# Fused sliding-window attention and squared-ReLU MLP on one core: first up-projection group in 128-token pieces, weights loaded between the first blocks, more transposes through the DMA

## Chip, cores, metric

The kernel runs on one core of a Trainium2 chip. The metric is device time in microseconds (us) of that core. Every kernel was run several times; executions of one kernel mostly agree within 1%, and all ratios here are of runs in the fast state (an execution over 1.5% above the fastest of its kernel counts as slow). A ratio is the mean time of one kernel's fast runs over the mean of the fast runs of the kernel before in the same rounds on the same chip, so it is not quite the ratio of the medians that are quoted beside it.

## The reference, cut to what matters

```python
# q, k, v: (8 batches, 8 heads, 576 tokens, 64) float32
scores = q @ k.T / 8
bias   = slope[h] * -abs(i - j)             # ALiBi
mask   = (i - j >= 0) & (i - j < 128)       # sliding window
attn   = softmax(where(mask, scores + bias, -1e9)) @ v
x = attn.transpose(0, 2, 1, 3).reshape(4608, 512)
h = maximum(x @ w_in, 0) ** 2               # w_in  (512, 2048)
out = h @ w_out                             # w_out (2048, 512), float32 out
```

## The kernel before

The program works on 40 attention blocks (8 batches of 576 tokens: four blocks of 128 and one of 64) and on 9 MLP groups of 512 tokens. A block needs k and q with the head dimension on the partitions (`kqT`), and its result x with the model dimension on the partitions (`xT`). Both turns can be done in two ways: on TensorE (eight 128x128 transposes for k and q, four for x, then copies out of PSUM), or by a DMA transpose that SyncE issues. Two constants choose the way by block number. A planner in Python, with its own estimates of durations, fixes one static order of instructions; on the chip each engine runs its list in that order and stops where an operand is missing.

```python
FIRST = "b0 b1 b2 b3 b4 i0 i1 i2 i3 b5 b6 b7 b8 b9 o0 o1 o2 o3"   # order of the first loads
SPLIT = [(0, 512)]           # pieces of group 0's up-projection
KQ_DMA, X_DMA = 10, 13       # from these blocks on, k/q and x are turned by DMA
size = {"kq": 4, "v": 6, "kqT": 5, "P": 3, "x": 3}                  # ring sizes
# [...]
def load_block(m, key):      # k, q, v of a block: float32 -> bf16, from GpSimd's queue
    # [...]
    nc.gpsimd.dma_start(o, src[b, :, kb * 128:kb * 128 + n, :].rearrange("h s d -> s h d"))
# [...]
if kq_by_dma:                # turn(m)
    nc.sync.dma_start_transpose(kqT[sk.idx], kq[s_in[m, "k"].idx].rearrange("s t f -> s (t f)"))
else:                        # 8 TensorE transposes of 128x128, two copies
    nc.tensor.transpose(slot.tile[:, i * 128:(i + 1) * 128], kq[...][:, i // C, ...], ident)
# [...]
if x_by_dma:                 # mix(m)
    nc.sync.dma_start_transpose(xT[:, :, t0:t0 + n], xt[sx.idx][0:n, :])
else:                        # 4 TensorE transposes, one copy
    nc.tensor.transpose(slot_x.tile[:, c * 128:(c + 1) * 128], xt[sx.idx][:, ...], ident)
```

The loads of all blocks are issued in block order from GpSimd.

The softmax here doesn't subtract the row's maximum and nothing guards it: scores larger than these inputs give would overflow.

Of the kernel before, what the change touches and what calls it, by code (L numbers as in the profile page):

```python
# [14 lines left out]
class Task:  # L15


    __slots__ = ("engs", "key", "emit", "deps", "acq", "rel", "nout", "users",
                 "ready", "start", "end", "eng", "seq", "lat", "dma")

# [16 lines left out]
class Plan:  # L37
# [18 lines left out]
    def order(self):  # L56
        used = {tag: [] for tag in self.bufs}
        free = {}
        cand = {}
        left = {}  # L60
# [12 lines left out]
        def avail(t):  # L73
            at = t.ready
            more = {}
            for s in t.acq:
                if s.idx is not None:
                    continue
                u = used[s.tag]
                n = self.bufs[s.tag]  # L80
                more[s.tag] = more.get(s.tag, 0) + 1
                i = len(u) + more[s.tag] - 1 - n
                if i >= 0:
                    old = u[i]
                    if old.left:
                        return None
                    at = max(at, old.freed)
            return at

        done = []  # L90
        n_all = len(self.tasks)
        while len(done) < n_all:
# [20 lines left out]
            if t.dma is not None:  # L113
                at = max(st + dur + 900.0, self.dma_free)
                self.dma_free = at + t.dma
                t.end = self.dma_free + 900.0
            else:
                t.end = st + dur + (self.LAT[e] if t.lat is None else t.lat)
            free[e] = st + dur
            for x in t.engs:  # L120
# [21 lines left out]
def kernel(  # L142
# [17 lines left out]

    FIRST = "b0 b1 b2 b3 b4 i0 i1 i2 i3 b5 b6 b7 b8 b9 o0 o1 o2 o3"
    SPLIT = [(0, 512)]

    KQ_DMA, X_DMA = 10, 13

# [3 lines left out]

    ident = const.tile([128, 128], BF16)  # L170
    masks = const.tile([128, H, 2, 128], BF16)
    pair_masks = const.tile([128, H, 256], BF16)
# [9 lines left out]


    size = {"kq": 4, "v": 6, "kqT": 5, "P": 3, "x": 3}
    kq = ring("kq", size["kq"], [128, 2, d_model])
# [16 lines left out]


    def build_iota():
        nc.gpsimd.iota(dist, pattern=[[-128, 2], [1, 128]], base=128, channel_multiplier=-1,
                       allow_small_or_imprecise_dtypes=True)

    t_iota = plan.add({"POOL": 360.0}, -9e5 + 0.012, build_iota)

    def build_ident():  # L210
        nc.vector.tensor_single_scalar(ident, dist[:, 1], 0.0, op=ALU.is_equal)

    t_ident = plan.add({"DVE": 230.0}, -9e5 - 1, build_ident, [t_iota])

# [19 lines left out]

    def build_pair():
        nc.vector.tensor_copy(pair_masks[:, :, 0:128].rearrange("p h (t s) -> p h t s", t=2), masks[:, :, :, 0:64])
        nc.vector.tensor_copy(pair_masks[:, :, 128:256], masks[:, :, 1, :])
        nc.vector.memset(kqT[NKB - 1][:, 0:C, 64:128], 0.0)

    t_pair = plan.add({"DVE": 1300.0}, -9e5 + 9, build_pair, t_mask)  # L240

    def ones():
        for t in vt:
            nc.vector.memset(t[:, :, D:D + 1], 1.0)
        for t in vt[NKB - 1:]:
            nc.vector.memset(t[64:128, :, 0:D], 0.0)
    t_ones = plan.add({"DVE": 1200.0}, -9e5 + 1, ones)


    def load(key, ns, emit, deps=(), acq=()):  # L250
        return plan.add({"POOL": 900.0}, key, emit, deps, acq, dma=ns)
# [21 lines left out]
    def load_block(m, key):  # L273
        b, kb = divmod(m, NKB)
        n = blk[kb]
        s_in[m, "k"] = s_in[m, "q"] = Slot("kq")
        s_in[m, "v"] = Slot("v")
        for i, (nm, src) in enumerate((("k", k), ("q", q), ("v", v))):
            sl = s_in[m, nm]

            def emit(i=i, src=src, sl=sl, nm=nm):
                o = (vt[sl.idx][0:n, :, 0:D] if nm == "v"
                     else kq[sl.idx][0:n, i].rearrange("s (h d) -> s h d", h=H))
                nc.gpsimd.dma_start(o, src[b, :, kb * 128:kb * 128 + n, :].rearrange("h s d -> s h d"))  # L284
            t_in[m, nm] = load(key + 0.01 * i, 1050.0 * n / 128, emit, [t_ones] if nm == "v" else [], [sl])

# [15 lines left out]
    def where(m):  # L302
        b, kb = divmod(m, NKB)
        return b, kb, blk[kb], (b * S + kb * 128 + blk[kb]) / 4 - 192 - 40, b == 0

    def turn(m):
# [7 lines left out]
        if kq_by_dma:  # L314
            def turn_kq():
                nc.sync.dma_start_transpose(kqT[sk.idx], kq[s_in[m, "k"].idx].rearrange("s t f -> s (t f)"))
            t_kq = [plan.add({"SP": 1300.0}, due - 80, turn_kq, [t_in[m, "k"], t_in[m, "q"]], [sk],
                             [s_in[m, "k"]], dma=1300.0)]
        else:
            slot = Slot("h" if first else "a")  # L320
            last = None
# [20 lines left out]
    def score(ms):  # L342
# [36 lines left out]
        for i in range(4):  # L379
            def view(t):  # L380
                if pair:
                    return t
                return t.rearrange("p c (t q) -> p c t q", t=2)[:, :, lo // 128:2, 0:n]

            def Pv(i=i):
                return view(Pt[sP.idx][:, 2 * i:2 * i + 2].rearrange("p h t q -> p h (t q)"))

            def expo(i=i):
                nc.scalar.activation(Pv(i), view(slot_s[i].tile.rearrange("p (c x) -> p c x", c=2)),  # L389
                                     AF.Exp, bias=0.0, scale=scale)  # L390
            cols = 2 * sum(w[2] for w in work_of)
            te = plan.add({"ACT": act(cols)}, due - 28 + 3 * i, expo, [tm], [], [slot_s[i]])

            def mask(i=i):
                pt = Pv(i)
                mk = (pair_masks if pair else masks.rearrange("p h t q -> p h (t q)"))[:, 2 * i:2 * i + 2]
                nc.vector.tensor_tensor(pt, pt, view(mk), op=ALU.mult)  # L397
            t_P.append(plan.add({"DVE": dve(cols, 2)}, due - 28 + 3 * i, mask,
                                [te] + (([t_pair] if pair else t_mask))))

    def mix(m):
# [57 lines left out]
        else:  # L459
            slot_x = Slot("h" if first else "a")  # L460
            last = None
# [31 lines left out]

    def fc_step(g, fc, key, lo=0, hi=512):
        if g not in g_slots:
            g_slots[g] = Slot("g")
            g_sq[g] = [[] for _ in range(FCB)]
        sg = g_slots[g]
        slot = Slot("o" if g == 0 and fc % 2 else "h")
        last = None  # L500
        w = hi - lo
        for cc in range(C):
            def emit(cc=cc, slot=slot):
                if cc == 0:
                    slot.tile = psum.tile([128, 512], FP32, tag=slot.tag, name="h")
                nc.tensor.matmul(slot.tile[:, 0:w], w_in_sb[:, cc, fc * 128:(fc + 1) * 128],  # L506
                                 xT[:, cc, g * 512 + lo:g * 512 + hi], start=cc == 0, stop=cc == C - 1)
            last = plan.add({"PE": mm(w)}, key + cc * w / 512, emit,
                            [last, t_win[fc // 4]] + tokens(g * 512 + lo, g * 512 + hi),
                            [slot, sg] if cc == 0 else [])  # L510
        srt = Slot("rt")

        def relu(slot=slot, srt=srt):
            srt.tile = work.tile([128, 512], BF16, tag="rt", bufs=3, name="rt")
            nc.scalar.activation(srt.tile[:, 0:w], slot.tile[:, 0:w], AF.Relu, bias=0.0, scale=1.0)  # L515
        tr = plan.add({"ACT": act(w)}, key, relu, [last], [srt], [slot])

        def square(srt=srt):
            if sg.tile is None:
                sg.tile = work.tile([128, FCB, 512], BF16, tag="g", bufs=2, name="g")  # L520
            nc.vector.tensor_tensor(sg.tile[:, fc, lo:hi], srt.tile[:, 0:w], srt.tile[:, 0:w], op=ALU.mult)  # L521
        g_sq[g][fc].append(plan.add({"DVE": dve(w, 2)}, key, square, [tr], [], [srt]))

    o_slots = {}

    def t_part(g, t, part, key):
# [4 lines left out]
        for fc in range(4 * part, 4 * part + 4):  # L531
            def emit(fc=fc):
                if fc == 0:
                    slot.tile = psum.tile([128, 512], FP32, tag="o", name="o")
                nc.tensor.matmul(slot.tile, sg.tile[:, fc, t * 128:(t + 1) * 128], w_out_sb[:, fc, :],  # L535
                                 start=fc == 0, stop=fc == FCB - 1)
            last = plan.add({"PE": mm(512)}, key + fc % 4, emit, [last, t_wout[fc // 4]] + g_sq[g][fc],
                            [slot] if fc == 0 else [], [sg] if t == 3 and fc == FCB - 1 else [])
        o_slots[g, t][1] = last
        if part == 3:  # L540
# [14 lines left out]
            plan.add({"SP": 350.0}, key, store, [te], [], [so])  # L555

    key = 0
    for lo, hi in SPLIT:
        for fc in range(FCB):
            fc_step(0, fc, key, lo, hi)  # L560
            key += 4 * (hi - lo) / 512
    for g in range(NG):
        for u in range(16):
            if g + 1 < NG:
                fc_step(g + 1, u, key)
                key += 4
            t_part(g, u // 4, u % 4, key)
            key += 4

    done = plan.order()  # L570
    kernel.plan = done
    with tc.manual_schedule():
# [32 lines left out]
```

## Time and profile before

| | before |
|---|---|
| time, median | 320.3 us |
| span of the profiled run | 318.9 us |
| first up-projection matmul | 24.05 us |
| last matmul starts | 314.7 us |
| TensorE idle after 40 us, by the waits | 0.8 us |

The waits of TensorE after 40 us (who waited, for whom, us in total, times, longest), kernel before:

```profile
PE h L506 <- DMA xT<-x: 0.6, 1, 0.6
PE xp L466 <- DVE x L447: 0.2, 1, 0.2
```

The DMA view of 40 to 140 us, kernel before: queue, packets, MB, share of the 16 engines (GpSimd's loads are `software_dynamic`, SyncE's stores and transposes `hardware_dynamic`); and for the DMA transposes the count and the median us from issue to landing:

```profile
q0 software_dynamic: 56860, 8.57, 137.2%
q1 hardware_dynamic: 22858, 7.90, 47.0%
...
kqT<-kq SPq DMA_TRANSPOSE x17, 6.3
...
xT<-x SPq DMA_TRANSPOSE x9, 6.3
```

A sum that is not a view of the profile is used below too: each matmul of the trace counted at its full-clock spacing as the trace shows it in full stretches (215.7 ns for 512 columns, 82 for 192, 56 for 128, 34 for a score of 128 columns, 30 for a P-times-v matmul; warm-up matmuls count as nothing), the total being TensorE's *work*. Time up to the last matmul less that work is *lost*. Half-speed windows count as lost in it. Before: 291.1 us of work, 23.6 us lost, 19.2 of them before 40 us and 2.8 from 40 to 140 us.

### The profile page before, as it was taken

How to read it: one execution, taken by the hardware profiler on the slowest of the kernel's cores; microseconds unless marked ns; L12 is line 12 of the kernel's file. 1: busy time of each engine (PE TensorE's matmuls, PEld its weight loads, DVE VectorE, ACT ScalarE, POOL GpSimd, SP SyncE). 2: the span in 40 equal slices, each digit the busy share in tenths (PEclk: the TensorE clock that was granted, in tenths of full speed). 3: DMA queues.
4: the chain of work that ended last, by engine and by line, in shares of the span. 5: the costliest groups of instructions: out<-in, count | busy, mean ns of one | idle time of the engine just before them, and what ended most of it. 6: DMA issues, size and time to landing. Idle time of an engine off the chain costs nothing.

```text
span 318.9 us, 6368 instructions
## 1 busy us (share of the span) xinstructions
PE 303.5 (95%) x2436; PEld 154.0 (48%) x2436; DVE 166.9 (52%) x476; ACT 176.2 (55%) x330; POOL 107.3 (34%) x133
## 2 busy tenths in 40 slices
PE   2779999999999999999999999999999999999995
PEld 1654555455555545444444454444544454444442
DVE  4782786367468655555545565555545563222200
ACT  4654874476386764555655573555655563444311
POOL 8974956157436336233442334221100000000000
PEclk9997999999999999999999999999999999999999
DMA  9999999999999999989997999996921111000121
GB/s 69 146 183 175 170 201 160 180 137 178 192 156 136 176 186 160 175 115 134 151 168 103 118 121 149 169 117 99 143 56 52 49 51 42 35 33 33 44 90 66
DMA packets 166783, 39.22 MB, mean 123 GB/s; under 512 B 158048, under 2 KB 162144, under 8 KB 166752
## 3 DMA queue, kind: packets, MB, share of 16 engines
q0 software_dynamic: 116736, 18.36, 85.4%
q1 hardware_dynamic: 50016, 20.46, 32.2%
q8 instruction: 19, 0.31, 0.4%
q14 instruction: 12, 0.10, 0.1%
HBM read 36.70 MB, written 9.44 MB: 145 GB/s over the span
## 4 chain that ended last, share of the span: by engine, by line
PE 91%; DMA 3%; DVE 2%; POOL 1%; issue 1%; ACT 1%; POOLq 0%; ACTq 0%
PE h L506 39%; PE o L535 39%; PE ps_s L370 6%; PE pv L419 5%; DMA xT<-x 2%; PE tp L326 1%; DMA kq<-in_q_dram 1%; PE xp L466 1%; POOL kq L284 1%; DVE x L447 1%; DVE P L397 1%; DVE kqT L298 1%; ACT kqT L300 0%; DVE xT L298 0%; POOL vt L284 0%
## 5 line engine op out<-in xcount | busy, mean ns | idle before, releaser
L506 PE MATMUL h<-xT,w_in_sb 128*128 128x512 bf16 x576 | 148.3, 382 | 1.1 <-DMA xT<-x 0.6
L535 PE MATMUL o<-w_out_sb,g 128*128 128x512 bf16 x576 | 147.2, 379 | 0.0
L515 ACT ACTIVATE rt<-h 128x512 bf16<-128x512 f32 x144 | 86.1, 605 | 97.7 <-PE h L506 92.5
L521 DVE TENSOR_TENSOR g<-rt 128x512 bf16<-128x512 bf16 x144 | 60.3, 420 | 83.9 <-ACT rt L515 82.8
L506 PEld LDWEIGHTS <-w_in_sb 128*128 128x128 bf16 x576 | 53.6, 98 | 59.8 <-issue 3.9
L535 PEld LDWEIGHTS <-g 128*128 128x128 bf16 x576 | 52.5, 98 | 56.4
L389 ACT ACTIVATE P<-ps_s 128x512 bf16<-128x512 f32 (+1 forms) x132 | 68.1, 593 | 13.8 <-PE ps_s L370 13.7
L284 POOL DMA_DIRECT2D kq<-in_k_dram x40 | 34.3, 859 | 70.3 <-DMA kqT<-kq 65.0
L284 POOL DMA_DIRECT2D vt<-in_v_dram x40 | 34.2, 858 | 47.8 <-PE pv L419 31.0
L397 DVE TENSOR_TENSOR P<-P,masks 128x512 bf16<-128x512 bf16 (+1 forms) x104 | 42.2, 411 | 14.7 <-ACT P L389 10.5
L419 PEld LDWEIGHTS <-P 128*128 128x128 bf16 x576 | 27.9, 99 | 17.5 <-DVE P L397 1.3
L284 POOL DMA_DIRECT2D kq<-in_q_dram x40 | 34.2, 856 | 3.4 <-PE h L506 1.7
L447 DVE TENSOR_TENSOR x<-pv,rec 128x256 bf16<-128x256 f32 (+1 forms) x80 | 33.2, 419 | 1.7
L546 ACT ACTIVATE osb<-o 128x512 f32<-128x512 f32 x36 | 21.6, 599 | 19.2 <-PE o L535 19.2
L419 PE MATMUL pv<-vt,P 128*128 128x65 bf16 x576 | 31.1, 195 | 0.7 <-DVE P L397 0.3
L442 DVE RECIPROCAL rec<-pv 128x4 f32<-128x4 f32 (+1 forms) x80 | 14.1, 179 | 18.2 <-PE pv L419 15.9
L370 PEld LDWEIGHTS <-kqT 64*128 64x128 bf16 x576 | 15.8, 97 | 14.9 <-issue 12.5
L370 PE MATMUL ps_s<-kqT 64*128 64x128 bf16 (+1 forms) x320 | 19.5, 218 | 0.8 <-DVE kqT L298 0.8
L370 PE MATMUL ps_s<-kqT,kqT 64*128 64x128 bf16 (+1 forms) x256 | 18.8, 217 | 1.1 <-DVE kqT L298 1.1
L326 PE MATMUL tp<-ident,kq 128*128 128x128 bf16 x80 | 8.4, 255 | 6.6 <-DMA kq<-in_k_dram 5.0
L397 DVE TENSOR_TENSOR P<-P,pair_masks 128x512 bf16<-128x512 bf16 x28 | 11.8, 424 | 5.3 <-ACT P L389 3.9
L326 PEld LDWEIGHTS <-kq 128*128 128x128 bf16 x80 | 6.2, 115 | 8.2 <-DMA kq<-in_k_dram 5.3
(25 smaller groups left out, 39.4 us busy)
## 6 DMA issues: line engine op xcount, KB each, us to landing
out_dram<-osb SPq DMA_DIRECT2D x36, 256.0 KB, 2.7
kq<-in_k_dram POOLq DMA_DIRECT2D x32, 128.0 KB, 5.4
kq<-in_q_dram POOLq DMA_DIRECT2D x32, 128.0 KB, 5.8
vt<-in_v_dram POOLq DMA_DIRECT2D x32, 128.0 KB, 5.8
w_in_sb<-in_moe_w_in_dram POOLq DMA_DIRECT2D x4, 512.0 KB, 9.9
w_out_sb<-in_moe_w_out_dram POOLq DMA_DIRECT2D x4, 512.0 KB, 10.1
kq<-in_k_dram POOLq DMA_DIRECT2D x8, 64.0 KB, 3.7
kq<-in_q_dram POOLq DMA_DIRECT2D x8, 64.0 KB, 4.1
```

The costliest lines, as they stand in the source:

```text
L284: nc.gpsimd.dma_start(o, src[b, :, kb * 128:kb * 128 + n, :].rearrange("h s d -> s h d"))
L326: nc.tensor.transpose(slot.tile[:, i * 128:(i + 1) * 128], kq[s_in[m, "k"].idx][:, i // C, (i % C) * 128:(i % C + 1) * 128], ident)
L370: nc.tensor.matmul(slot_s[2 * (c // 2) + half].tile.rearrange("p (c x) -> p c x", c=2)[:, c % 2, at:at + w], kqT[sk_of[mk].idx][rows, c, : ...
L389: nc.scalar.activation(Pv(i), view(slot_s[i].tile.rearrange("p (c x) -> p c x", c=2)), AF.Exp, bias=0.0, scale=scale)
L397: nc.vector.tensor_tensor(pt, pt, view(mk), op=ALU.mult)
L419: nc.tensor.matmul(slot_v.tile[:, hi * (D + 1):(hi + 1) * (D + 1)], Pt[sP.idx][:, place(h)].rearrange("p t q -> p (t q)")[:, at_of[m, part ...
L447: nc.vector.tensor_tensor(xt[sx.idx][0:n, hf * 256:(hf + 1) * 256].rearrange("p (h e) -> p h e", h=4), pv[0:n, :, 0:D], srec.tile[0:n, :]. ...
L506: nc.tensor.matmul(slot.tile[:, 0:w], w_in_sb[:, cc, fc * 128:(fc + 1) * 128], xT[:, cc, g * 512 + lo:g * 512 + hi], start=cc == 0, stop=c ...
L515: nc.scalar.activation(srt.tile[:, 0:w], slot.tile[:, 0:w], AF.Relu, bias=0.0, scale=1.0)
L521: nc.vector.tensor_tensor(sg.tile[:, fc, lo:hi], srt.tile[:, 0:w], srt.tile[:, 0:w], op=ALU.mult)
L535: nc.tensor.matmul(slot.tile, sg.tile[:, fc, t * 128:(t + 1) * 128], w_out_sb[:, fc, :], start=fc == 0, stop=fc == FCB - 1)
L546: nc.scalar.activation(so.tile, slot.tile, AF.Copy)
```

## The change

The intent is to shorten the start: begin the up-projection before all 512 tokens of group 0 and all weights are there, and take turns off TensorE. The core of the diff, cut:

```diff
-    FIRST = "b0 b1 b2 b3 b4 i0 i1 i2 i3 b5 b6 b7 b8 b9 o0 o1 o2 o3"
-    SPLIT = [(0, 512)]
+    FIRST = "b0 b1 b2 i0 b3 i1 b4 i2 b5 b6 o0 i3 o1 o2 o3 b7 b8 b9"
+    SPLIT = {0: [(0, 128), (128, 256), (256, 384), (384, 512)], 1: [(0, 192), (192, 320), (320, 512)]}
+    EARLY = -80
+    AHEAD = {10: -60, 11: -30, 6: -60, 7: 60, ...}     # cut: shifts of single blocks
+    LEAD = 20
-    KQ_DMA, X_DMA = 10, 13
+    KQ_DMA, X_DMA = 7, 5
+    WARM = 6                                            # matmuls on zeros at the start
-    size = {"kq": 4, "v": 6, "kqT": 5, "P": 3, "x": 3}
+    size = {"kq": 4, "v": 6, "kqT": 6, "P": 2, "x": 4}
     # [...] load_block, first block only:
+                nc.sync.dma_start(kq32[:, i]..., src[b, :, ...])   # fp32, no cast, SyncE's queue
     # [...] turn, first block only: fp32 transposes of kq32 with ident32
     # [...] fc_step: one PSUM bank holds 4 (or 2) slices of a 128- (192-) token piece
```

More of the change, by code (lines that the diff above doesn't have):

```diff
@@ L18 @@
     __slots__ = ("engs", "key", "emit", "deps", "acq", "rel", "nout", "users",
-                 "ready", "start", "end", "eng", "seq", "lat", "dma")
+                 "ready", "start", "end", "eng", "seq", "lat", "dma", "rs", "rs_end", "re", "cols", "fill")
     def __init__(self, engs, key, emit, deps=(), acq=(), rel=(), lat=None, dma=None):
@@ L58, in order @@
         free = {}
+        lanes = {"SP": [], "POOL": []}
         cand = {}
@@ L74, in avail @@
             at = t.ready
+            if t.dma is not None or t.engs.get("SP"):
+                e = next(iter(t.engs))
+                if len(lanes[e]) >= 8:
+                    at = max(at, lanes[e][-8])
             more = {}
@@ L88, in avail @@
             return at
+        self.used = used
         done = []
@@ L116, in order @@
                 t.end = self.dma_free + 900.0
+                lanes[e].append(t.end)
             else:
                 t.end = st + dur + (self.LAT[e] if t.lat is None else t.lat)
+                if e == "SP":
+                    lanes[e].append(t.end)
             free[e] = st + dur
@@ L159 @@
     NBLK = B * NKB
-    FIRST = "b0 b1 b2 b3 b4 i0 i1 i2 i3 b5 b6 b7 b8 b9 o0 o1 o2 o3"
-    SPLIT = [(0, 512)]
-    KQ_DMA, X_DMA = 10, 13
+    FIRST = "b0 b1 b2 i0 b3 i1 b4 i2 b5 b6 o0 i3 o1 o2 o3 b7 b8 b9"
+    SPLIT = {0: [(0, 128), (128, 256), (256, 384), (384, 512)], 1: [(0, 192), (192, 320), (320, 512)]}
+    EARLY = -80
+    AHEAD = {10: -60, 11: -30, 6: -60, 7: 60, 4: 0, 1: 90, 2: 0, 3: 30, 5: 90, 9: -30, 12: 90, 8: 60, 0: 60}
+    LEAD = 20
+    KQ_DMA, X_DMA = 7, 5
+    WARM = 6
     const = ctx.enter_context(tc.tile_pool(name="const", bufs=1))
@@ L170 @@
     ident = const.tile([128, 128], BF16)
+    ident32 = const.tile([128, 128], FP32)
+    kq32 = const.tile([128, 2, d_model], FP32)
+    zero = const.tile([128, 512], BF16)
     masks = const.tile([128, H, 2, 128], BF16)
@@ L206, in build_iota @@
                        allow_small_or_imprecise_dtypes=True)
-    t_iota = plan.add({"POOL": 360.0}, -9e5 + 0.012, build_iota)
+    t_iota = plan.add({"POOL": 360.0}, -9.1e5, build_iota)
     def build_ident():
-        nc.vector.tensor_single_scalar(ident, dist[:, 1], 0.0, op=ALU.is_equal)
-    t_ident = plan.add({"DVE": 230.0}, -9e5 - 1, build_ident, [t_iota])
+        nc.vector.tensor_single_scalar(ident32, dist[:, 1], 0.0, op=ALU.is_equal)
+        nc.vector.tensor_copy(ident, ident32)
+    t_ident = plan.add({"DVE": 350.0}, -9e5 - 1, build_ident, [t_iota])
     def build_dist():
@@ L233, with pair_rest, pair_own, zero_task @@
         t_mask.append(plan.add({"ACT": act(256)}, -9e5 + h, build_mask, [t_dist]))
-    def build_pair():
+    later = []
+    def pair_rest():
         nc.vector.tensor_copy(pair_masks[:, :, 0:128].rearrange("p h (t s) -> p h t s", t=2), masks[:, :, :, 0:64])
+    def pair_own():
         nc.vector.tensor_copy(pair_masks[:, :, 128:256], masks[:, :, 1, :])
-        nc.vector.memset(kqT[NKB - 1][:, 0:C, 64:128], 0.0)
-    t_pair = plan.add({"DVE": 1300.0}, -9e5 + 9, build_pair, t_mask)
+    t_pair = [plan.add({"DVE": 340.0}, -9e5 + 9, f, later + t_mask) for f in (pair_rest, pair_own)]
     def ones():
+        nc.vector.memset(zero, 0.0)
         for t in vt:
             nc.vector.memset(t[:, :, D:D + 1], 1.0)
-        for t in vt[NKB - 1:]:
-            nc.vector.memset(t[64:128, :, 0:D], 0.0)
-    t_ones = plan.add({"DVE": 1200.0}, -9e5 + 1, ones)
+    t_ones = plan.add({"DVE": 450.0}, -9.1e5, ones)
+    def zero_task(o, n):
+        def emit():
+            nc.vector.memset(o, 0.0)
+        task = plan.add({"DVE": dve(n)}, -9e5 + 9, emit, [t_ones])
+        return task
+    t_zeros = {}
+    def zero_first(nm, ring_, cut, n):
+        if len(ring_) > NKB - 1:
+            t_zeros[nm] = zero_task(cut(ring_[NKB - 1]), n)
+    zero_first("v", vt, lambda t: t[64:128, :, 0:D], 512)
+    zero_first("kq", kq, lambda t: t[64:128], 512)
+    zero_first("kqT", kqT, lambda t: t[:, 0:C, 64:128], 128)
+    def warm():
+        t = psum.tile([128, 512], FP32, tag="a", bufs=plan.bufs["a"], name="warm")
+        for i in range(WARM):
+            nc.tensor.matmul(t, zero[:, 0:128], zero, start=True, stop=True)
+    sw = Slot("a")
+    plan.add({"PE": 427.0 * WARM}, -9.1e5, warm, [t_ones], [sw], [sw])
     def load(key, ns, emit, deps=(), acq=()):
@@ L275, in load_block @@
         n = blk[kb]
+        wide = m == 0
         s_in[m, "k"] = s_in[m, "q"] = Slot("kq")
@@ L279, in load_block, with emit32 @@
             sl = s_in[m, nm]
+            if wide and nm != "v":
+                def emit32(i=i, src=src):
+                    nc.sync.dma_start(kq32[:, i].rearrange("s (h d) -> s h d", h=H),
+                                      src[b, :, kb * 128:kb * 128 + n, :].rearrange("h s d -> s h d"))
+                t_in[m, nm] = plan.add({"SP": 450.0}, key + 0.01 * i, emit32, dma=870.0)
+                continue
             def emit(i=i, src=src, sl=sl, nm=nm):
@@ L284, in emit @@
                 nc.gpsimd.dma_start(o, src[b, :, kb * 128:kb * 128 + n, :].rearrange("h s d -> s h d"))
-            t_in[m, nm] = load(key + 0.01 * i, 1050.0 * n / 128, emit, [t_ones] if nm == "v" else [], [sl])
+            deps = [t_ones] if nm == "v" else []
+            if n < 128:
+                deps.append(t_zeros.get("v" if nm == "v" else "kq"))
+            t_in[m, nm] = load(key + 0.01 * i, 870.0 * n / 128, emit, deps, [sl])
     for i, what in enumerate(FIRST.split()):
@@ L303, in where @@
         b, kb = divmod(m, NKB)
-        return b, kb, blk[kb], (b * S + kb * 128 + blk[kb]) / 4 - 192 - 40, b == 0
+        return b, kb, blk[kb], (b * S + kb * 128 + blk[kb]) / 4 - 192 - 40 - AHEAD.get(m, LEAD if m >= X_DMA else 0), b == 0
     def turn(m):
@@ L318, in turn, with emit, evac @@
                              [s_in[m, "k"]], dma=1300.0)]
+        elif m == 0:
+            t_kq = []
+            for i in range(2):
+                slot = Slot("o")
+                last = None
+                for c in range(C):
+                    def emit(i=i, c=c, slot=slot):
+                        if c == 0:
+                            slot.tile = psum.tile([128, 512], FP32, tag="o", name="tp")
+                        nc.tensor.transpose(slot.tile[:, c * 128:(c + 1) * 128],
+                                            kq32[:, i, c * 128:(c + 1) * 128], ident32)
+                    last = plan.add({"PE": mm(128)}, due - 56, emit,
+                                    [last, t_ident, t_in[m, "kq"[i]]] + chain["tp"],
+                                    ([slot] + ([sk] if i == 0 else [])) if c == 0 else [])
+                chain["tp"] = [last]
+                def evac(i=i, slot=slot):
+                    copy(t_kq[i], kqT[sk.idx][:, i * C:(i + 1) * C, 0:n],
+                         slot.tile.rearrange("p (c s) -> p c s", c=C)[:, :, 0:n])
+                t_kq.append(plan.add({"ACT": act(C * n), "DVE": dve(C * n)}, due - 56, evac, [last], [], [slot]))
         else:
-            slot = Slot("h" if first else "a")
+            slot = Slot("o" if first else "a")
             last = None
@@ L398, in score @@
             t_P.append(plan.add({"DVE": dve(cols, 2)}, due - 28 + 3 * i, mask,
-                                [te] + (([t_pair] if pair else t_mask))))
+                                [te] + (t_pair if pair else [t_mask[h] for h in range(H) if place(h) // 2 == i])))
     def mix(m):
@@ L459, in mix @@
         else:
-            slot_x = Slot("h" if first else "a")
+            slot_x = Slot("o" if first else "a")
             last = None
@@ L492, with fc_step @@
     g_slots, g_sq = {}, {}
-    def fc_step(g, fc, key, lo=0, hi=512):
+    def fc_step(g, unit, key, lo=0, hi=512):
         if g not in g_slots:
@@ L498, in fc_step @@
         sg = g_slots[g]
-        slot = Slot("o" if g == 0 and fc % 2 else "h")
-        last = None
-        w = hi - lo
-        for cc in range(C):
-            def emit(cc=cc, slot=slot):
-                if cc == 0:
-                    slot.tile = psum.tile([128, 512], FP32, tag=slot.tag, name="h")
-                nc.tensor.matmul(slot.tile[:, 0:w], w_in_sb[:, cc, fc * 128:(fc + 1) * 128],
-                                 xT[:, cc, g * 512 + lo:g * 512 + hi], start=cc == 0, stop=cc == C - 1)
-            last = plan.add({"PE": mm(w)}, key + cc * w / 512, emit,
-                            [last, t_win[fc // 4]] + tokens(g * 512 + lo, g * 512 + hi),
-                            [slot, sg] if cc == 0 else [])
+        w = hi - lo
@@ new lines, in fc_step, with emit @@
+        per = 512 // w
+        slot = Slot("h")
+        fcs = range(unit * per, min(FCB, (unit + 1) * per))
+        cols = len(fcs) * w
+        last = None
+        for fi, fc in enumerate(fcs):
+            for cc in range(C):
+                def emit(cc=cc, fc=fc, fi=fi):
+                    if cc == 0 and fi == 0:
+                        slot.tile = psum.tile([128, 512], FP32, tag=slot.tag, name="h")
+                    nc.tensor.matmul(slot.tile[:, fi * w:(fi + 1) * w], w_in_sb[:, cc, fc * 128:(fc + 1) * 128],
+                                     xT[:, cc, g * 512 + lo:g * 512 + hi], start=cc == 0, stop=cc == C - 1)
+                last = plan.add({"PE": mm(w)}, key + (fi * C + cc) * w / 512, emit,
+                                [last, t_win[fc // 4]] + tokens(g * 512 + lo, g * 512 + hi),
+                                [slot, sg] if cc == 0 and fi == 0 else [])
@@ L511, in fc_step, with relu @@
         srt = Slot("rt")
-        def relu(slot=slot, srt=srt):
+        def relu():
             srt.tile = work.tile([128, 512], BF16, tag="rt", bufs=3, name="rt")
-            nc.scalar.activation(srt.tile[:, 0:w], slot.tile[:, 0:w], AF.Relu, bias=0.0, scale=1.0)
-        tr = plan.add({"ACT": act(w)}, key, relu, [last], [srt], [slot])
-        def square(srt=srt):
+            nc.scalar.activation(srt.tile[:, 0:cols], slot.tile[:, 0:cols], AF.Relu, bias=0.0, scale=1.0)
+        tr = plan.add({"ACT": act(cols)}, key, relu, [last], [srt], [slot])
@@ L519, in square @@
+        def square():
             if sg.tile is None:
                 sg.tile = work.tile([128, FCB, 512], BF16, tag="g", bufs=2, name="g")
-            nc.vector.tensor_tensor(sg.tile[:, fc, lo:hi], srt.tile[:, 0:w], srt.tile[:, 0:w], op=ALU.mult)
-        g_sq[g][fc].append(plan.add({"DVE": dve(w, 2)}, key, square, [tr], [], [srt]))
+            r = srt.tile[:, 0:cols].rearrange("p (f w) -> p f w", f=len(fcs))
+            nc.vector.tensor_tensor(sg.tile[:, fcs[0]:fcs[-1] + 1, lo:hi], r, r, op=ALU.mult)
@@ L524 @@
+        ts = plan.add({"DVE": dve(cols, 2)}, key, square, [tr], [], [srt])
+        for fc in fcs:
+            g_sq[g][fc].append((lo, hi, ts))
     o_slots = {}
@@ L536, in emit @@
                                  start=fc == 0, stop=fc == FCB - 1)
-            last = plan.add({"PE": mm(512)}, key + fc % 4, emit, [last, t_wout[fc // 4]] + g_sq[g][fc],
+            last = plan.add({"PE": mm(512)}, key + fc % 4, emit, [last, t_wout[fc // 4]] + [x for lo, hi, x in g_sq[g][fc] if lo < (t + 1) * 128 and hi > t * 128],
                             [slot] if fc == 0 else [], [sg] if t == 3 and fc == FCB - 1 else [])
@@ L555, in t_part, with steps @@
             plan.add({"SP": 350.0}, key, store, [te], [], [so])
+    def steps(g):
+        return [(u, lo, hi) for lo, hi in SPLIT.get(g, [(0, 512)]) for u in range(-(-FCB // (512 // (hi - lo))))]
     key = 0
-    for lo, hi in SPLIT:
-        for fc in range(FCB):
-            fc_step(0, fc, key, lo, hi)
-            key += 4 * (hi - lo) / 512
+    for u, lo, hi in steps(0):
+        fc_step(0, u, key, lo, hi)
+        key += 64 / len(steps(0))
     for g in range(NG):
+        todo = steps(g + 1) if g + 1 < NG else []
+        each = 64 / max(1, len(todo))
         for u in range(16):
-            if g + 1 < NG:
-                fc_step(g + 1, u, key)
-                key += 4
+            for x in todo[u * len(todo) // 16:(u + 1) * len(todo) // 16]:
+                fc_step(g + 1, x[0], key + (EARLY if g == 0 else 0), *x[1:])
+                key += each
             t_part(g, u // 4, u % 4, key)
@@ L570 @@
     done = plan.order()
-    kernel.plan = done
     with tc.manual_schedule():
```

## The prediction

> **What bounds it now.** From 24.05 to 315.1 us TensorE is the bound: in the waits, its idle time after 40 us is under 1 us, and the chain of waits is matmuls only. The last 3.8 us are eviction and store. The loss is at the start: by the timeline, 168 matmul instructions of attention run before 24.05 us, at full-clock spacings (transpose 56 ns, score 34, pv 30) 6.7 us of work; 17 us are lost. Another 1.7 us go because the page's clock row grants half speed from 24.0 to 27.4 us, when up-projection starts. The Trainium skill ("TensorE: Matmul & The Clock Gate", Part 1) says that the gate judges windows of about 3.4 us by activity; the trace agrees: few matmuls from 20 to 24 us, then 3.41 us at half clock. Lost: 19 us.
>
> Loads set that start. k, q, v of a block land about 0.88 us apart (first k at 4.78 us, q at 6.1), the quarters of the up-weights 2.55 us apart (21.9, 24.5, 27.1, 29.7; read off GpSimd's issue waits). Up-projection also waits for all 512 tokens; VectorE is 75-100% busy from 14 to 23 us.
>
> **What the change does.**
> 1. First k and q come uncast through SyncE; GpSimd starts with iota and v: block 0 is ready 1.5 to 2 us earlier.
> 2. Weights between blocks: estimated from the spacings, quarter 0 lands near 14 us instead of 22, quarter 1 near 19, quarter 2 near 23, quarter 3 near 33 (behind blocks 5, 6 and first down-weights).
> 3. Group 0's up-projection in 128-token pieces: a piece with one quarter is 16 x 56 = 0.9 us; 256 matmuls of 56 ns for 64 of 216: +0.5 us. From 14 to 24 us 6 to 7 pieces fill idle TensorE time and help the clock. Blocks 3 and 4 come later, and from 23 to 29 us I expect thin stretches (2-3 us). From 29 us the engine is full. Lost: 10 us before 14 us, 4 to 5 after, clock included, in place of 19: gain 4 to 5 us.
> 4. Transposes of k, q of blocks 7-9 and x of blocks 5-12 move to SyncE's queue: (24 + 32) x 56 ns = 3.1 us off the saturated TensorE, all on the chain. It adds 11 DMA transposes (5.0-5.3 us to landing) to a DMA that is full until 200 us; some land late and stall TensorE for 1 us (estimate).
> 5. Warm-up matmuls, fp32 transposes and memsets lie in idle time; the smaller P ring costs little. Tail unchanged.
>
> Sum: -4.5 (start) -3.1 (transposes) +0.5 (short matmuls) +1 (stalls) = -6, up to -10 with better filling; I take -7.8.
>
> **Predicted: 312.5 us, range 307 to 317.5.** Faster by over 2%: 0.60; within 2%: 0.38; slower by over 2%: 0.02.
>
> **What would show it.** Timeline: first 128-column up-projection near 14 us. Windows from 14 to 24 us: mainly up-projection. Clock row: no half-speed stretch after 17 us, or a shorter one. Groups: k/q transposes 56 instead of 80, x transposes 20 instead of 52. Waits: TensorE idle after 40 us under 2 us, else step 4 is wrong. Last matmul near 307.
>
> **What would make it wrong.** Faster: first q by 3.5 us and quarter 0 by 12 us, so the engine is full from 14 us. Slower: VectorE and ScalarE are the true limit there and the added relu and square delay attention; quarter 3 at 33 us blocks the in-order stream; late DMA transposes stall groups 1 and 2; or fp32 loads crowd the same engines and delay v and block 1.

## More of the kernel before

A k/q buffer (`kq`, four of them) is held from the issue of its load until its turn is done.

The profiled run cut into stretches of 20 us gives, per stretch, its length, TensorE's busy time with its count of matmuls, the granted TensorE clock, the busy share of the DMA engines (it can exceed 1, as transfers of several queues overlap) and the GB/s that they moved. Kernel before:

```profile
0.00:20.00 20.00, 11.29 (x146) 1.00 1.59 119
20.00:40.00 20.00, 17.98 (x155) 0.91 1.85 179
40.00:60.00 20.00, 19.79 (x191) 1.00 1.90 181
60.00:80.00 20.00, 20.00 (x172) 1.00 1.61 161
80.00:100.00 20.00, 20.00 (x205) 1.00 1.71 171
100.00:120.00 20.00, 19.39 (x184) 1.00 2.23 165
120.00:140.00 20.00, 20.00 (x154) 1.00 1.78 154
```

TensorE has only 11.3 busy us in the first 20 and is nearly full from 40 us on. The GB/s column says the other thing that matters here: the DMA runs at 150 to 180 GB/s from 20 to 140 us. The clock column reads 1.00 also where the trace has no clock record. It has none before 17.19 us, and there 128x128 transposes start 107 ns apart, against 56 ns later: TensorE ran at half speed, in the kernel after too (until 17.42 us).

## The result, and the profile after

The median after is 328.85 us (327.84 to 329.7) against 320.76 us before in the same rounds; ratio 1.0251, interval 1.0214 to 1.0288. It is 2.5% slower, where 2.4% faster was forecast.

The same stretches, kernel after:

```profile
0.00:20.00 20.00, 15.99 (x164) 1.00 1.61 153
20.00:40.00 20.00, 18.88 (x370) 1.00 1.57 193
40.00:60.00 20.00, 18.32 (x164) 1.00 2.12 146
60.00:80.00 20.00, 18.32 (x246) 1.00 2.08 160
80.00:100.00 20.00, 16.61 (x192) 1.00 1.71 163
100.00:120.00 20.00, 19.27 (x173) 1.00 1.92 160
120.00:140.00 20.00, 15.30 (x129) 0.91 1.87 181
```

Read against the table of before: the first two stretches gain 4.7 and 0.9 busy us (the six warm-up matmuls are 2.7 us of the first gain, and most of the first stretch is at half speed in both kernels, so busy time there is not work). From 40 us on the stretches are no longer full: 80 to 100 us has 3.4 us of idle TensorE, 120 to 140 us has 4.7 and a clock of 0.91 of full speed, which is one window of 3.4 us at half speed that begins as the longest stall ends. After 140 us both kernels are full.

The waits of TensorE after 40 us, kernel after:

```profile
PE ps_s L439 <- DMA kqT<-kq: 8.8, 4, 4.3
PE h L579 <- DMA xT<-x: 1.7, 2, 1.2
PE o L611 <- DMA w_out_sb<-in_moe_w_out_dram: 1.7, 2, 1.2
```

12.2 us of waits, all for DMA transfers, where there were 0.6: four for turned k/q, two for turned x, two for down-weights. The DMA view of 40 to 140 us, kernel after:

```profile
q0 software_dynamic: 55303, 7.10, 130.4%
q1 hardware_dynamic: 28046, 8.94, 62.9%
...
kqT<-kq SPq DMA_TRANSPOSE x19, 8.4
...
xT<-x SPq DMA_TRANSPOSE x14, 7.9
```

SyncE's queue moved 1.04 MB more than before, GpSimd's 1.47 MB less, and the sum is no larger. The 1.47 MB are not loads of k, q and v that were pushed out: they are the down-weights, which the new order moves mostly before 40 us. Counted by size in the trace (not a view of the profile), the packets of k, q and v, 128 bytes each, are 54,261 before and 54,186 after in this window. Up to 40 us they are 26,112 before and only 17,933 after (and 2,048 for block 0 in float32): at 3,072 packets a block, the kernel after enters the window two blocks behind, and does not make up for them there. So the loads are late: q of block 18 was issued at 76.7 us before and at 92.6 us after. And a transpose now takes 8 us from issue to landing in place of 6.3. One stall in full. The timeline of SyncE's queue in the kernel after (start, length of the issue, what):

```profile
84.10 3.60 SPq L365 DMA_TRANSPOSE kqT<-kq  x1
```

The timeline of TensorE in the same kernel (start, length, what; in brackets the idle time before it and what ended it):

```profile
90.82 0.19 PE L439 MATMUL ps_s<-kqT 64*128 64x64 bf16 x2
94.40 0.23 PE L439 MATMUL ps_s<-kqT 64*128 64x128 bf16 x2 [3.39 <-DMA kqT<-kq]
```

The k/q transpose issued at 84.10 us lands at 94.35 by the chain of waits, 10.25 us later, and TensorE stands from 91.0 to 94.4 us in the middle of a score burst, because its list is in order.

In the sum from the trace:

| us | before | after | difference |
|---|---|---|---|
| TensorE work | 291.1 | 288.8 | -2.3 |
| lost before 40 us | 19.2 | 15.1 | -4.1 |
| lost from 40 to 140 us | 2.8 | 16.2 | +13.4 |
| lost after 140 us | 1.6 | 1.6 | 0 |
| last matmul starts | 314.7 | 321.7 | +7.0 |

So the start did become shorter. The question of the experiments is what the 13.4 us are.

### The profile page after: what moved, and what is told of

Same layout as the page of the kernel before. It is cut to its first block, busy times and chain, and to the rows that moved or that the text cites. A ratio compares the mean times of both kernels' runs of the same rounds, so it can differ in the third digit from the quotient of the medians.

```text
span 326.1 us, 6946 instructions
## 1 busy us (share of the span) xinstructions
PE 304.8 (93%) x2706; PEld 169.0 (52%) x2706; DVE 163.5 (50%) x469; ACT 176.1 (54%) x332; POOL 105.8 (32%) x131
## 4 chain that ended last, share of the span: by engine, by line
PE 65%; DMA 26%; POOL 5%; SPq 1%; issue 1%; ACT 0%; DVE 0%; ACTq 0%; POOLq 0%
PE o L611 30%; PE h L579 29%; DMA kqT<-kq 9%; DMA w_out_sb<-in_moe_w_out_dram 5%; DMA kq<-in_q_dram 5%; DMA xT<-x 4%; PE pv L488 3%; DMA w_in_sb<-in_moe_w_in_dram 3%; PE ps_s L439 3%; POOL kq L330 2%; POOL vt L330 1%; SPq L365 1%; POOL w_out_sb L305 1%; POOL w_in_sb L298 0%; ACT osb L622 0%
## 5 line engine op out<-in xcount | busy, mean ns | idle before, releaser
L579 PE MATMUL h<-xT,w_in_sb 128*128 128x512 bf16 (+2 forms) x896 | 153.7, 305 | 2.6 <-DMA xT<-x 1.7
L611 PE MATMUL o<-w_out_sb,g 128*128 128x512 bf16 x576 | 148.9, 381 | 1.7 <-DMA w_out_sb<-in_moe_w_out_dram 1.7
L588 ACT ACTIVATE rt<-h 128x512 bf16<-128x512 f32 (+1 forms) x148 | 86.6, 592 | 86.1 <-PE h L579 73.3
L595 DVE TENSOR_TENSOR g<-rt 128x512 bf16<-128x512 bf16 (+1 forms) x148 | 61.3, 414 | 86.1 <-ACT rt L588 84.8
L579 PEld LDWEIGHTS <-w_in_sb 128*128 128x128 bf16 x896 | 70.4, 99 | 49.8 <-issue 1.8
L611 PEld LDWEIGHTS <-g 128*128 128x128 bf16 x576 | 53.8, 98 | 60.1 <-issue 3.6
L458 ACT ACTIVATE P<-ps_s 128x512 bf16<-128x512 f32 (+1 forms) x132 | 69.2, 592 | 26.4 <-PE ps_s L439 26.4
L330 POOL DMA_DIRECT2D kq<-in_k_dram x39 | 32.9, 844 | 86.0 <-DMA kqT<-kq 78.9
L395 PE MATMUL tp<-ident,kq 128*128 128x128 bf16 x48 | 4.7, 250 | 0.1
L349 ACT ACTIVATE kqT<-tp 128x512 bf16<-128x512 bf16 (+1 forms) x5 | 2.8, 564 | 2.4 <-DVE kqT L347 1.6
```

What stands on the lines that cost most here:

```text
L458: nc.scalar.activation(Pv(i), view(slot_s[i].tile.rearrange("p (c x) -> p c x", c=2)), AF.Exp, bias=0.0, scale=scale)
L579: nc.tensor.matmul(slot.tile[:, fi * w:(fi + 1) * w], w_in_sb[:, cc, fc * 128:(fc + 1) * 128], xT[:, cc, g * 512 + lo:g * 512 + hi], start ...
L588: nc.scalar.activation(srt.tile[:, 0:cols], slot.tile[:, 0:cols], AF.Relu, bias=0.0, scale=1.0)
L595: nc.vector.tensor_tensor(sg.tile[:, fcs[0]:fcs[-1] + 1, lo:hi], r, r, op=ALU.mult)
L611: nc.tensor.matmul(slot.tile, sg.tile[:, fc, t * 128:(t + 1) * 128], w_out_sb[:, fc, :], start=fc == 0, stop=fc == FCB - 1)
```

## Experiments

Twelve kernels ran. Theory 1 was that the 11 added DMA transposes overload the DMA; later, as theory A, in the sharper form that DMA *throughput* is short from 40 to 140 us. Rivals: the new load order and the rings (theory 2), and latency through the four k/q buffers and SyncE's in-order queue (theory B).

### 1. Turns back on TensorE, all else as after

```diff
-    KQ_DMA, X_DMA = 7, 5
+    KQ_DMA, X_DMA = 10, 13
```

> The kernel after, with the transposes of k, q of blocks 7 to 9 and x of blocks 5 to 12 back on TensorE; all else as after. Theory 1 (the 11 added DMA transposes overload the DMA between 35 and 80 us and the loads never catch up): TensorE's idle time after 40 us falls from about 12 us to under 3, time 313 to 317 us, below the kernel before. Theory 2 (the load order and rings make the loads late, whatever does the transposes): stalls stay, 325 us or more.

Measured: 321.48 us against 320.84 before; ratio 1.0032 (0.9991 to 1.0073). Better than after by 7 us, but not the 313 to 317 that were expected. In place of the four stalls over 1 us that after has there is one, in TensorE's timeline:

```profile
110.60 1.24 PE L611 MATMUL o<-w_out_sb,g 128*128 128x512 bf16 x5 [0.16 <-issue]
114.70 1.46 PE L579 MATMUL h<-xT,w_in_sb 128*128 128x512 bf16 x4 [2.86 <-issue]
```

The profile puts this wait down to "issue", that is, to nothing that it shows. The x transpose issued at 106.45 us landed at 114.61 by the trace, 0.09 us before that matmul starts, while the two waits that the trace records for the matmul had ended by 112.97. So it too looks like a late DMA, though the wait itself is not among the records (some 40 matmul records are missing here). A window at half clock follows, as after the longest stall in the kernel after. So the early start alone, with the turns of before, uses up the slack that the loads had: the gain of some 4 us comes, and goes again at 114 us.

Two things in this trace say what the turns cost. Its transposes take as long to land as those of the kernel after (8.4 us for k/q, 7.8 for x, from 40 to 140 us), so the longer landing alone is not what the 11 turns brought. But it enters the window as far behind with its loads (17,982 packets of k, q and v up to 40 us) and then moves 59,528 of them, where after moves 54,186: with the turns on TensorE the loads can catch up. (The clock at the start varies between runs: this one was at full speed from 5.9 to 9.3 us and at half speed from there to 19.6; after was at half speed until 17.4.)

### 2. The moved turns alone, on the kernel before

```diff
-    KQ_DMA, X_DMA = 10, 13
+    KQ_DMA, X_DMA = 7, 5
```

> The kernel before with only the transposes of blocks 7 to 9 (k, q) and 5 to 12 (x) moved to SyncE's queue. Theory 1: loads lag and TensorE stalls on kqT after 40 us, time 326 us or more. Theory 2: the 3.1 us off TensorE show, 317 to 319 us.

Measured: 335.23 us, ratio 1.0449 (1.0403 to 1.0496). This one part, which the prediction booked as a gain of 2 us, costs 14.4 us by itself. TensorE's longest waits after 40 us in this kernel:

```profile
PE o L535 <- DMA w_out_sb<-in_moe_w_out_dram: 6.6, 2, 5.1
PE ps_s L370 <- DMA kqT<-kq: 5.6, 1, 5.6
```

The clock record adds to them: half speed from 49.6 to 56.4 us and from 70.1 to 83.7, of which 8.6 us lie in the stalls themselves. Here the load order is that of before, so the DMA view of 40 to 140 us can be set against the one of before (22,858 packets and 7.90 MB from SyncE's queue, 56,860 and 8.57 MB from GpSimd's):

```profile
q0 software_dynamic: 49040, 7.58, 121.5%
q1 hardware_dynamic: 26989, 8.46, 57.5%
```

More from SyncE's queue, fewer loads from GpSimd's. Part of the second may be feedback (not separated here): while TensorE stands, buffers come free later, and so loads are issued later.

### 3. The old load order, all else as after

```diff
-    FIRST = "b0 b1 b2 i0 b3 i1 b4 i2 b5 b6 o0 i3 o1 o2 o3 b7 b8 b9"
+    FIRST = "b0 b1 b2 b3 b4 i0 i1 i2 i3 b5 b6 b7 b8 b9 o0 o1 o2 o3"
```

> The kernel after with the order of the first 18 loads of before. Theory 1: stalls after 40 us stay (8 us or more idle), time 326 us or more. Theory 2, in the form that down-weights ahead of blocks 7 to 9 start the lag: blocks 7 to 9 are loaded 8 us sooner and stalls nearly go, 320 us or less, in spite of a later first up-projection.

Measured: 334.47 us over four runs, one of them slow; the three fast ones took 330.79 to 335.2 us, ratio 1.0389 (1.0324 to 1.0454). Going back to the old order is no cure; with these turns it is worse. Why it is worse stays open: its profiled run was slow, and its trace is not used.

### 4. The old ring sizes, all else as after

```diff
-    size = {"kq": 4, "v": 6, "kqT": 6, "P": 2, "x": 4}
+    size = {"kq": 4, "v": 6, "kqT": 5, "P": 3, "x": 3}
```

> The kernel after with the ring sizes of before (kqT 5, P 3, x 3). Theory 1: within 2 us of after (327 to 331). Theory 2, in the form that the smaller P ring holds attention back: stalls shrink, under 324 us.

Measured: 330.01 us, ratio 1.0279 (1.0239 to 1.032), the same as after within the intervals. The three rings changed together, so what the smaller P ring costs by itself is not shown; the new sizes as a whole cost nothing that can be seen.

### 5. Thin v loads

From block 7 on each v load brings one head of eight. The instructions, their order, the rings, the transposes and the SyncE queue stay; DMA work goes. Two things about the size of this cut: it takes away 26,432 packets in all, against the 6,912 that the moved turns added (counted below), and GpSimd's own time to issue a v load falls too, from 0.89 to 0.56 us. The second is a rival that no run separates; GpSimd is busy for 32% of the span of the kernel after, so it is an unlikely one. The result is wrong.

```diff
+                if nm == "v" and m >= 7:
+                    nc.gpsimd.dma_start(vt[sl.idx][0:n, 0:1, 0:D],
+                                        src[b, 0:1, kb * 128:kb * 128 + n, :].rearrange("h s d -> s h d"))
+                    return
```

> The kernel after, wrong result on purpose: from block 7 on each v load brings one head of eight, so the same instructions, order and rings, but about 0.77 us less DMA work per block (7/8 of 0.88). Theory A (DMA throughput is short between 40 and 140 us): the landing times of the transposes fall from about 8 us to under 6 and TensorE's lost time from 40 to 140 us falls from 16 to under 4 us, time 313 to 318 us. Theory B (latency: four k/q buffers, each held from the issue of the load until the DMA transpose lands, and SyncE's in-order queue): mostly unchanged, 325 us or more.

Measured: 314.41 us, ratio 0.983 (0.9791 to 0.987). The stalls from 60 us on are gone; one of 1.5 us for down-weights, at 45.8 us, stays. Stretches from 40 us, kernel after with thin v:

```profile
40.00:60.00 20.00, 18.47 (x169) 1.00 1.81 153
60.00:80.00 20.00, 20.00 (x283) 1.00 1.82 184
80.00:100.00 20.00, 20.00 (x212) 1.00 1.80 193
100.00:120.00 20.00, 20.00 (x196) 1.00 1.92 164
120.00:140.00 20.00, 20.00 (x168) 1.00 1.62 159
```

The only wait of TensorE after 40 us:

```profile
PE o L615 <- DMA w_out_sb<-in_moe_w_out_dram: 1.5, 1, 1.5
```

Its transposes land sooner, although SyncE issues more of them in the same 40 to 140 us:

```profile
kqT<-kq SPq DMA_TRANSPOSE x22, 5.5
...
xT<-x SPq DMA_TRANSPOSE x17, 5.9
```

With the 11 moved transposes in place and room on the DMA, the kernel comes within 2 us of the time that was predicted for it (312.5).

### 6. Control: thin v loads on the kernel before

The same edit on the kernel before.

> Control: the kernel before with the same thinned v loads (wrong on purpose). TensorE there loses under 3 us from 40 to 140 us, so if thin loads help only where DMA is short, this kernel gains little: 317 to 321 us. If thin loads save time by something else (start-up, the last stores), it gains some 10 us as the kernel after did.

Measured: 319.95 us, ratio 0.9966 (0.9905 to 1.0028): the same. So less DMA work is worth some 14 us where the turns were moved and nothing that can be seen where they were not.

### 7. Six k/q buffers, all else as after

```diff
-    size = {"kq": 4, ...
+    size = {"kq": 6, ...
```

> The kernel after with 6 k/q buffers instead of 4. Theory A (throughput): little changes, 325 to 330 us, the landing times grow further. Theory B (latency through the four buffers): GpSimd's wait for kqT falls well below 79 us and the time to 320 us or less.

Measured: 331.02 us, ratio 1.0339 (1.0309 to 1.0369). GpSimd's wait for `kqT`, 78.9 us in the kernel after, fell to 9.0 us, and the time did not fall. The waits of TensorE after 40 us in this kernel, where the late transfer is now mostly x:

```profile
PE h L579 <- DMA xT<-x: 8.1, 3, 4.1
PE ps_s L439 <- DMA kqT<-kq: 2.5, 3, 1.3
```

The loads are issued earlier and then take 14.4 us to land in place of 8.7 (median of the k loads from 40 to 140 us). The four buffers look like the limit in the list of waits, and are not. The other half of theory B, SyncE's in-order queue, is left as it was in experiment 5, and the stalls go. So theory B falls.

### 8. Only x moved

```diff
-    KQ_DMA, X_DMA = 7, 5
+    KQ_DMA, X_DMA = 10, 5
```

> The kernel after with only x of blocks 5 to 12 moved to SyncE's queue (k, q of 7 to 9 back on TensorE). If the number of DMA transposes counts (8 of 11 added here, the smaller ones), 325 to 327 us; if it is the k/q transposes, which hold the k/q buffers, 321 to 323 us as with both undone.

Measured: 326.23 us, ratio 1.0207 (1.0157 to 1.0257). The eight x transposes hold no k/q buffer and still bring most of the loss. (They are 3,840 of the 6,912 added packets; one kernel in between is too little to say that the loss is in proportion to them.)

### 9. More turns on TensorE than before

```diff
-    KQ_DMA, X_DMA = 7, 5
+    KQ_DMA, X_DMA = 15, 18
```

> The kernel after with k, q of blocks up to 14 and x of blocks up to 17 turned on TensorE (DMA transposes from 15 and 18; before had 10 and 13). Theory A: the stall near 112 us that the version with 10 and 13 kept (4 us with its half clock) goes, for 60 transposes of 56 ns = 3.4 us more work: 318 to 321 us, no stall over 1 us after 40 us. Theory B: the same direction but it can't be told apart here; if a stall stays, the early start itself outruns the loads.

Measured: 319.2 us, ratio 0.9979 (0.9946 to 1.0012). No stall over 1 us after 40 us; by the sum from the trace 295.2 us of work and 19.6 lost, against 291.1 and 23.6 before. The shorter start is all there, and is spent on 4 us of work, 3.4 of them the 60 further transposes (estimate, 60 x 56 ns).

### 10 to 12. How few turns on TensorE are enough

The same line, with 10 and 17, 10 and 21, 12 and 21.

> After with 10 and 17: half of that relief for 0.9 us of TensorE work. 316 to 318 us if it is enough, 319 to 321 if the stall stays.

Measured: 317.58 us, ratio 0.9881 (0.983 to 0.9931).

> After with k, q transposes on DMA from block 10 and x transposes only from block 21: 8 x-turns of 4 x 56 ns = 1.8 us more TensorE work than with 10 and 13, for some 6 us less DMA work before 140 us. If DMA throughput is the cause, the stall at 112 us goes and the sum is 291.9 + 1.8 of work + 19 lost = last matmul at 313, time 317 to 318.5 us; if a stall stays, 320 or more.

Measured: 317.4 us, ratio 0.9881 (0.9828 to 0.9934).

> After with 12 and 21: 0.9 us more work than with 10 and 21 and 2 more k/q transposes off the DMA. No stall; 318 to 319 us, the sum of work and start, about 1 us over the version with 10 and 21 if that has no stall either.

Measured: 319.18 us, ratio 0.993 (0.9881 to 0.9979).

All three results are correct. The first two lie in the ranges named, the third 0.2 us above its range. With 10 and 17 no wait for a DMA is left in TensorE's waits after 40 us; what is left are gaps of 0.2 us, the length of one matmul. This trace holds 878 of 896 up-projection and 555 of 576 down-projection matmuls, so they are probably missing records:

```profile
PE h L579 <- issue: 1.7, 11, 0.2
PE o L611 <- issue: 0.5, 3, 0.2
```

Turning four more blocks' x on TensorE than before (blocks 13 to 16) makes the change 1.2% faster than the kernel before (an interval clear of 1, but inside the 2% within which two kernels count as the same), and some 11 us faster than the change as it was made (medians of different rounds).

## Why the prediction was wrong

- *"From 24.05 to 315.1 us TensorE is the bound"*: right as a reading, and wrong as a base. TensorE was full because the loads ran just ahead of it. The DMA's row, full until about 200 us, was read and even named, and no one asked how much it could still take. The row cannot say that: with 10 and 17 it also reads 9 in 39 of the 40 slices from 40 to 140 us, and there no wait for a DMA is left.
- *Steps 1 to 3, the start (-4.5, +0.5)*: right. 4.1 us less lost before 40 us; the first 128-column up-projection started at 15.55 us (14 was said); no half-speed window from 17.4 us until the one at 123.2 us that follows a stall.
- *Step 4, the work taken off TensorE (-3.1)*: right; together with the shorter matmuls the work fell by 2.3 us (-2.6 was said).
- *Step 4, "some land late and stall TensorE for 1 us (estimate)"*: **this is the step that failed**: the cost of the added DMA work was mis-sized. The lost time from 40 to 140 us grew by 13.4 us. The prediction's own test ("TensorE idle after 40 us under 2 us, else step 4 is wrong") gave 12.2 us, and the moved turns alone cost 14.4 us (experiment 2). The term was sized by nothing. It could have been: the trace of before has 43,008 packets of 256 bytes for 30 k/q transposes and 27 of x, which is 1,024 for a k/q transpose, 512 for x of a full block and 256 for x of a half one; so the 11 moved transposes are 6,912 packets; the DMA moved 79,730 packets in the 100 us from 40 to 140, 1.25 ns each; the estimate is 8.7 us if the DMA had no room at all. It is rough, since packets differ and since 79,730 was not a ceiling: the kernel with 10 and 17 moved 87,446 in the same window. But it says that the term is not small. The loads behind the transposes come later, and the new start, which takes the down-weights first and is two blocks behind with k, q and v at 40 us, needs room to catch up.
- *Step 5, rings*: not contradicted; by experiment 4 the three new sizes together cost nothing that can be seen.
- The mechanism is shown by experiments 2, 5, 6 and 7 together: adding transposes alone makes the loss, taking DMA work away removes all stalls but one of 1.5 us, the same relief on the kernel before does nothing, and more buffers do nothing. The Trainium skill says why two queues can displace each other ("DMA: Bandwidth & Descriptors", section "SWDGE vs HWDGE vs iDMA"): each of the 16 DMA engines holds queues of both issuers and takes turns between them. The traces agree as far as they go: before and experiment 2 have the same load order, and with 0.56 MB more through SyncE's queue from 40 to 140 us, GpSimd's moved 0.99 MB less, perhaps in part by feedback. No run here shows the taking of turns itself.

Two more things are worth keeping. The forecast time was that of a kernel whose DMA has room: with thin v loads it takes 314.4 us. And the clock adds to a stall. The Trainium skill ("TensorE: Matmul & The Clock Gate", Part 1) says that the clock falls to half after an idle window of about 3.4 us, and that these windows run freely, whatever the kernel does. The trace of after agrees: its half-speed window begins 31 steps of 3.413 us after its first clock record, at 123.23 us; the stall from 119.27 to 123.54 covered the whole step before it, and 3.4 us at half clock cost some 1.7 us on top. The stall of 3.39 us at 91.0 us fell across two steps (1.50 and 1.89 us) and cost no clock. In experiment 1 a stall of 2.86 us, within one step and so less than a whole idle window, was enough. So it is not the length alone that decides.

Open: what exactly the DMA is short of, since with 10 and 17 it moved more packets and more bytes from 40 to 140 us (87,446 and 16.61 MB) than in the kernel after (83,360 and 16.19 MB), and still nothing waited; why the old load order is worse with these turns; and which of the start's parts (pieces, order, fp32 first block, warm-up) brings how much of the 4.1 us. The shifts of single blocks (`EARLY`, `AHEAD`, `LEAD`) and the pieces of group 1 also changed when TensorE wants which block, and no run varied them.

## What to carry to other kernels

Moving work from the engine that is full to one that looks free is a gain only if the other has room in that stretch of time; for a DMA, a rough size is the packets of the moved transfers against the packets per microsecond that the trace already shows there. A DMA row that is full and on which nobody waits does not say how near the limit is. Here it hid a second bound close behind the first, and an earlier start and a few more transfers made it the first. An experiment that takes DMA work away, on both kernels, tells. A long wait in the list (79 us for four buffers) is not proof that buffers are short; more buffers only moved the wait into the transfers.

## What the Trainium skill lacked or had wrong

- "DMA: Bandwidth & Descriptors" gives a bandwidth for DMA transposes (261 GB/s in one kernel), but not what a transpose between two on-chip buffers takes while loads are in flight: here the k/q transposes took 5.3 us median from issue to landing in the kernel before and 8.1 in the kernel after, and the quickest x transpose 2.3.
- The same page says that software- and hardware-issued transfers take turns on the engines, but not how long a load is delayed by it. Here the moved turns alone (experiment 2) took the median landing from 40 to 140 us from 5.8 to 6.3 us for the full k loads, from 6.2 to 7.9 for q and from 6.3 to 7.3 for v.
- "TensorE: Matmul & The Clock Gate", Part 4, gives times for a bf16 transpose only. At half clock, 128x128 transposes of fp32 started 0.213 us apart here, and those of bf16 0.107 us.
